# Attention and gated feed-forward on one core: the first chunk's attention and first feature steps in halves of 256 queries, and output stores ahead of transposes in SyncE's queue

## The chip, the core and the metric

The kernel runs on one NeuronCore of a Trainium2 chip. The metric is the device time of one execution in microseconds (us). Executions of one kernel agree within some 0.3%, so the effect here, about 1.2 us in 276, needs several runs of both kernels on the same chip. All numbers are from fast runs, unless a run is said to be a single one of unknown state.

## The reference

```python
scores = q @ k^T / 8                       # 4 batches, 8 heads, 768 positions, 64 per head
mask   = causal for heads 0, 2, 6 ("retrieval");
         the 4 first keys and a window of 64 for the other five ("streaming")
x      = softmax(scores) @ v               # -> 3072 tokens x 512
g, val = x @ w_gate, x @ w_val             # 512 -> 1536
y      = (gelu(g) * val) @ w_out           # 1536 -> 512
out    = x + sigmoid(x @ w_res) * y
```

## The kernel before

The 3072 tokens are worked in six chunks of 512. A chunk's attention makes `xT` (its output, transposed to features by tokens); then follow twelve feature steps f = 0 to 11, each with four gate and four value matmuls of 512 columns, GELU on ScalarE and a product on VectorE; then the output.

Nothing is ordered by hand. The program adds tasks with an engine, an assumed duration, dependencies and a priority (lower goes first), and a list scheduler, at build time, fixes the order of instructions on every engine. `HINTS` replaces priorities by task number; it was found by a search for this set of tasks, so its numbers mean something else as soon as a task is added. `.late` adds to the assumed landing time of a transfer: it changes no transfer, only the order that the scheduler chooses.

```python
P_ps = Psum(psum, {            # PSUM: 8 banks; kind: (slots at once, the banks of each)
    "av1": (2, one(0, 1)), "av2": (1, [(0, 1)]), "av0": (3, [(0, 1), (6, 7), (2, 3)]),
    ...
    "gv": (4, one(6, 7, 5, 4, 3, 2)), "gv0": (4, one(6, 7, 5, 4)), "gv00": (2, one(6, 7)), ...
})
P_ot = Pool(many("otile", 3, [128, D_MODEL], FP32))      # three output tiles
...
def load_weights():                                      # all issued on GpSimd's queue
    ...                                                  # wg, wv in 3 pieces: priority -20 + j
    wtok["r"] = dma("pool", -12, 2.6, ...)
    for j in range(4):
        wtok["o", j] = dma("pool", -11 + j, 1.95, ...)
...
def loads_rows(c, si, b, a, z):                          # chunks 0 and 1
    base = {0: -60, 1: -15, 2: 50}[c]
    ...                                                  # queries, keys: priority base + ...
    values(b, a, z, base + (10 if c == 0 else 8), False, c == 0)
...
# a chunk's feature steps: a matmul group needs all 512 queries
for f in range(NF):
    pr = 1000 * c + 500 + f
    kind = "gv" if f > 1 else "gv0" if c or f else "gv00"
    ...
# the store of an output tile, in SyncE's queue
G.add("sp", 0.6, ... e.dma_start(out[r0:r0 + 128, w], at(ot)[:, w]) ..., [t2], pr, bufs=[ot], dma=0.75, name="out")
...
# matmuls of a blank tile fill TensorE where nothing else is ready
G.add("pe", 0.06, ... e.matmul(at(warm)[:, 0:128], lhsT=blank[:, :], rhs=blank[:, :], ...), [t_blank], 1e9, ...)
...
for c, segs in enumerate(CHUNKS):
    attention(c, segs, xbuf, xtbuf, xtoks, xttoks)
    h, htoks = gate_value(c, xtbuf, xttoks)
    output(c, h, htoks, xbuf, xtoks, xtbuf, xttoks)
```

SyncE's queue also carries the transposes of later chunks' queries and keys, and the shift copies `vs <- va` (values moved by 64 rows for the window).

The softmax here doesn't subtract the row's maximum and nothing guards it: scores larger than these inputs give would overflow.

Of the kernel before, what the change touches and what calls it, by code (L numbers as in the profile page):

```python
# [42 lines left out]
    "3:-21.19 5:-58.49 6:-58.34 403:490.65 425:595.32 427:528.41 578:-99.99 586:59.9 611:1499.22 612:516.59 "  # L43
    "622:576.96 635:549.35 636:510.21 637:1538.66 643:580.14 647:570.57 648:558.53 649:1085.71 650:1520.19 "
    "653:525.88 654:576.91 655:1026.63 659:511.56 665:514.73 666:516.61 668:1537.73 671:15.77 673:62.65 "
    "677:0.03 679:80.17 680:-75.91 683:82.91 684:-86.3 685:102.37 686:529.24 689:511.01 701:88.3 702:-1.38 "
    "703:114.98 707:516.6 719:1104.93 722:2562.67 733:1538.65 734:1503.99 756:501.37 777:2386.85 816:2334.5 "
    "855:2510.01 861:1434.93 874:2134.02 886:2457.99 922:3352.32 923:1980.91 924:1487.38 972:2502.01 "
    "996:3513.25 1004:2538.32 1026:1534.33 1040:3534.81 1067:2441.52 1090:4509.27 1095:4498.99 1113:4499.01 "
    "1136:4429.99 1139:3502.04 1181:4467.35 1251:4123.82 1253:4130.53 1262:4510.02 1322:5341.74 1368:4505.02 "  # L50
    "1370:5425.02 1394:5537.53 1399:5528.12 1411:5499.01 1412:4524.63 1418:5505.02 1423:5573.53 1424:5090.24 "
    "1444:5424.01 1446:4529.17 1457:5122.53 1458:6525.69 1468:5116.43 1482:4952.05 1485:6442.5 1510:5505.99 "
    "1553:5511.01 1554:5505.99 1608:7485.06 1628:7447.37 1653:7483.11 "
# [391 lines left out]
def build_kernel(nc, q, k, v, w_gate, w_val, w_out, w_res, out):  # L445
# [34 lines left out]
        "av1": (2, one(0, 1)), "av2": (1, [(0, 1)]), "av0": (3, [(0, 1), (6, 7), (2, 3)]),  # L480
        "sc": (2, [(2, 3), (4, 5)]), "scr": (3, one(5, 4, 3, 2)), "scr0": (3, one(6, 5, 4, 3, 2)),
        "gv": (4, one(6, 7, 5, 4, 3, 2)), "gv0": (4, one(6, 7, 5, 4)), "gv00": (2, one(6, 7)), "out": (2, one(6, 7)), "warm": (1, one(7, 5, 1)),
# [56 lines left out]
    def load_weights():  # L539
        for j in range(3):  # L540
            for nm, t, src in (("g", wg, w_gate), ("v", wv, w_val)):
                s = slice(j * 512, (j + 1) * 512)
                wtok[nm, j] = dma("pool", -20 + j, 2.6, (lambda t=t, s=s: lambda: t[:, :, s])(),
                                  src[:, s].rearrange("(ci p) f -> p ci f", p=128))
        wtok["r"] = dma("pool", -12, 2.6, lambda: wr[:, :, :], w_res.rearrange("(ci p) f -> p ci f", p=128))
        for j in range(4):
            s = slice(j * 3, (j + 1) * 3)
            wtok["o", j] = dma("pool", -11 + j, 1.95, (lambda s=s: lambda: wo[:, s, :])(),
                               w_out[j * 384:(j + 1) * 384, :].rearrange("(fi p) c -> p fi c", p=128))

# [14 lines left out]
    def values(b, a, z, base, each, on_engines=False):  # L565
# [21 lines left out]
        if on_engines:  # L587
            ts = []
            for dst, src, off in ((0, 64, 1), (64, 0, 0)):
                def vs(on, dst=dst, src=src, off=off):  # L590
                    def fn(e):
                        o = at(BB.vs)[dst:dst + 64, a_ - 1:z - 1, :, :].rearrange("p i h d -> p (i h d)")
                        i_ = at(BB.v)[src:src + 64, a_ - off:z - off, :, :].rearrange("p i h d -> p (i h d)")
                        return e.activation(out=o, in_=i_, func=AF.Copy) if on == "act" else e.tensor_copy(out=o, in_=i_)
                    return fn
                n_ = (z - a_) * 520
                ts.append(G.flex({"dve": (c_dve(n_, 3.0, False), vs("dve")), "act": (c_act(n_), vs("act"))},
                                 [BB.vtok[i - off] for i in range(a_, z)], 130, bufs=[BB.v, BB.vs], name="vs"))
            for i in range(a_, z):
                BB.vstok[i] = ts  # L600
            late_copies.extend(ts)
            return
# [13 lines left out]
    def loads_rows(c, si, b, a, z):  # L616
# [18 lines left out]
        values(b, a, z, base + (10 if c == 0 else 8), False, c == 0)  # L635

        per = 1 if c == 0 or n == 4 else 2
        for k_ in range(0, NPAIR, per):
            ps_ = ORDER[k_:k_ + per]
            pr = 1000 * c - 492 + ps_[0] if c else 40 * k_ - 5  # L640
# [29 lines left out]
    def loads_natural(c, si, b, a, z):  # L670
# [5 lines left out]
        for i in range(a, z):  # L676
            for j, src in ((1, k), (0, q)):
# [6 lines left out]
                t = G.add("sp", 1.3, (lambda sv=sv, i=i, j=j: lambda e: e.dma_start(  # L684
# [11 lines left out]
    def attention(c, segs, xbuf, xtbuf, xtoks, xttoks):  # L696
        tiles = [(b, i) for (b, a, z) in segs for i in range(a, z)]
        todo = []
        for k_, p in enumerate(ORDER):
            P = B()  # L700
            P.heads, P.p, P.c, P.pr = PAIRS[p], p, c, 1000 * c + 40 * k_
# [23 lines left out]
        sinks = sink_scores(c, [t for t in tiles if t[1] > 0], 1000 * c + 40 + 5)  # L725
        for t in ph(c, "sc")[:-1]:
            if t.name[2:] in (str(ORDER[2]), str(ORDER[3])):
                t.order.append(ph(c, "sc")[-1])
# [9 lines left out]
        last, norms = None, []  # L738
        for P in todo:
# [3 lines left out]
            last, tn = weigh(P, tiles, sinks, xbuf, x16, xtoks, xdeps, last)  # L743
            if P.heads[0] % 2 == 1:
                for cb in (P.heads[0] // 2, P.heads[1] // 2):
                    to_features(c, cb, P.pr, x16, xdeps, xtbuf, xttoks)
                if P is todo[-1]:
                    tn.order += [t for _, t in xttoks[-2:]]
                if c == 0 and P is todo[-1]:
                    for t in norms[1:]:  # L750
                        t.order.append(xdeps[-1])
            norms.append(tn)

# [87 lines left out]
    def sink_scores(c, need, pr):  # L841

        S = B()
        S.where, S.four, S.et = {}, {}, Buf(P_ek)
        scr = Buf(P_ps, "sc")
        for m, (b, i) in enumerate(need):
            for h in (1, 3, 5, 7):
                S.where[h, b, i] = m * 128
            S.where[4, b, i] = 512
# [3 lines left out]
        cols = (need + need[-1:])[0:4]  # L853
# [13 lines left out]
        for j, (b, i) in enumerate(cols):  # L867
            mms.append((j, batch(b), slice(0, 64), 1, 512, i * 128, 128))

        def sc(e):  # L870
# [7 lines left out]
        S.txs = [G.add("act", c_act(640), lambda e: e.activation(  # L878
            out=at(S.et)[:, 0:640], in_=at(scr)[:, 0:640], func=AF.Exp, scale=SM_SCALE),
            [ts], pr, bufs=[scr, S.et], fset="exp", name="expk")]  # L880
# [3 lines left out]
    def weigh(P, tiles, sinks, xbuf, x16, xtoks, xdeps, last):  # L884
        n = len(tiles)
        c, pr, heads = P.c, P.pr, P.heads
        av = Buf(P_ps, "av2" if c else "av0")
# [3 lines left out]
        def windows(xs, lts):  # L891
            def fn(e):
                r = []
                for x in xs:
                    for lt in lts:
                        b, i = tiles[lt]
                        o, w, BB, h = x * 512 + lt * 65, P.where[x, None, b, i], batch(b), heads[x]
                        for s in range(2):
# [3 lines left out]
                                              start=lt == 0, stop=(i == 0), skip_group_check=True))  # L902
# [3 lines left out]
        def keys(x, lt):  # L906
            def fn(e):
                b, i = tiles[lt]
                o = x * 512 + lt * 65
                return [e.matmul(at(av)[:, o:o + 65], lhsT=at(P.et)[:, P.where[x, kt, b, i]:P.where[x, kt, b, i] + 128],  # L910
                                 rhs=at(batch(b).v)[:, kt, heads[x], :], start=lt == 0 and kt == 0, stop=(kt == i),
# [3 lines left out]
        def sinkf(x, h):  # L915
            def fn(e):
                r = []
                for lt, (b, i) in enumerate(tiles):
                    if i == 0:
                        continue  # L920
                    o, ko = x * 512 + lt * 65, sinks.where[h, b, i]
# [25 lines left out]
        def avv(d0, d1):  # L947
            return at(av).rearrange("p (x w) -> p x w", x=2)[:, :, 0:n * 65].rearrange(
# [8 lines left out]
        xview = lambda: at(xbuf)[:, 0:n, :].rearrange("p i (y x d) -> p x i y d", x=2, d=128)[:, :, :, heads[0] // 4, half]  # L957
        direct = c == 0 or heads[0] % 2
        if direct:

            xdeps.append(G.add("dve", c_dve(2 * n * 64), lambda e: e.tensor_tensor(
                out=at(x16)[:, :, :, half], in0=avv(0, DHEAD), in1=scale(), op=ALU.mult), [t1], pr - 2.5, bufs=[av, rc, x16], name="norm16"))
        t2 = G.add("dve", c_dve(2 * n * 64), lambda e: e.tensor_tensor(  # L963
            out=xview(), in0=avv(0, DHEAD), in1=scale(), op=ALU.mult), [t1] + xdeps, pr - 2 + (200 if c == 0 and heads[0] else 0), bufs=[av, rc, xbuf], name="norm")
        for i in range(n):
            xtoks.setdefault(i, []).append(t2)
        if not direct:
            def cast(on):
                return lambda e: (e.activation(out=at(x16)[:, :, :, half], in_=xview(), func=AF.Copy) if on == "act" else
                                  e.tensor_copy(out=at(x16)[:, :, :, half], in_=xview()))  # L970
# [4 lines left out]
    def to_features(c, cb, pr, x16, xdeps, xtbuf, xttoks):  # L975
        n = 4
# [5 lines left out]
        def ev(on):  # L982
            def fn(e):
                o, i_ = at(xtbuf)[:, cb, 0:n * 128], at16(scr)[:, 0:n * 128]
# [7 lines left out]
    def gate_value(c, xtbuf, xttoks):  # L992
# [4 lines left out]
        for f in range(NF):  # L997
            pr = 1000 * c + 500 + f
            kind = "gv" if f > 1 else "gv0" if c or f else "gv00"
# [20 lines left out]
            toks.append(th)  # L1020
# [3 lines left out]
    def output(c, h, htoks, xbuf, xtoks, xtbuf, xttoks):  # L1024
        segs = [(b, t) for (b, a, z) in CHUNKS[c] for t in range(a, z)]
        for lt in range(4):
# [14 lines left out]
            for w in ((slice(0, 256), slice(256, 512)) if last else (slice(0, 512),)):  # L1041
                fb = Buf(P_ps, "gv" if last else "out")
                n = w.stop - w.start
                for j in range(6):
# [3 lines left out]
                        [prev_t, wtok["o", j * 2 // 3], wtok["o", (2 * j + 1) // 3]] + htoks[2 * j:2 * j + 2], pr,  # L1048
# [6 lines left out]
                    [t1] + xtoks[lt], pr + (0 if c == len(CHUNKS) - 1 else 90), bufs=[ot, xbuf], name="add")  # L1055
                G.add("sp", 0.6, (lambda ot=ot, r0=r0, w=w: lambda e: e.dma_start(out[r0:r0 + 128, w], at(ot)[:, w]))(),
                      [t2], pr, bufs=[ot], dma=0.75, name="out")
# [13 lines left out]
    firsts = None  # L1071
    for t in late_copies:
        t.order += [x for d in (batches[0].ktok, batches[0].qtok) for (p, i), x in d.items() if i == 0]
    for c, segs in enumerate(CHUNKS):
        xbuf, xtbuf, xtoks, xttoks = Buf(P_x), Buf(P_xt), {}, []
        attention(c, segs, xbuf, xtbuf, xtoks, xttoks)
        firsts = firsts or xttoks
        h, htoks = gate_value(c, xtbuf, xttoks)
# [3 lines left out]
    for c in range(len(CHUNKS)):  # L1082
        gv, gelu = ph(c, "gv"), ph(c, "gelu")
        for f, t in gv:
            t.order += ph(c, "sc") + (ph(c, "xT") if f > (1 if c else 0) else [])
        for t in ph(c, "table"):
            t.order += ph(c, "exp") + ([x for _, x in firsts[:2]] if c == 0 else [])
# [65 lines left out]
```

## Time and profile before

| what | before | where it is read |
|---|---|---|
| median of 3 runs | 275.91 us (275.73 to 276.66) | run times |
| profiled span | 274.1 us | page |
| TensorE busy, 8.7 to 21.9 us | 12.52 of 13.2, of which blank 6.14 | windows |
| first feature matmul | 21.92 us | TensorE's timeline |
| TensorE's waits at the end of chunk 1's attention | 0.69 + 0.47 us | TensorE's timeline |

How to read it: TensorE is nearly always busy, so a saving must come from one of the few stretches where its work is blank or where it waits. There are two: the start, before the first feature step, and 67 to 70 us. The lines are in the prediction.

### The profile page before, as it was taken

Reading aid. Unit: us, or ns where it says so; the run is one execution under the profiler, and the core shown is the slowest. Engines: PE = TensorE matmul, PEld = TensorE weight load, DVE = VectorE, ACT = ScalarE, POOL = GpSimd, SP = SyncE. Lnnn points to the kernel's source line nnn. Section 1 sums busy time; section 2 is a strip of 40 time slices with the busy share of each in tenths; the row PEclk is TensorE's granted clock in tenths of the full one; section 3 lists DMA queues with packets and bytes.
Section 4 is the critical chain, followed back from the end, with each engine's and each line's share of the span. In section 5 each row is a group of like instructions: output and inputs, shape, how many; then the busy total and the mean of one; then the engine's idle time right before and its main releaser. Section 6 shows DMA issues by size and latency. Waiting matters only on the chain.

```text
span 274.1 us, 5645 instructions
## 1 busy us (share of the span) xinstructions
PE 267.2 (97%) x2398; PEld 138.5 (51%) x2398; DVE 139.6 (51%) x254; ACT 140.7 (51%) x205; POOL 86.2 (31%) x120
## 2 busy tenths in 40 slices
PE   7999999999999999999999999999999999999995
PEld 7774454454444465444455444455444456544443
DVE  2785353386433457435456544467525156743344
ACT  3744266775435876434773333776333778333410
POOL 8999259991382532992000000000000000000000
PEclk9999999999999999999999999999999999999999
DMA  6999999999999999999911000121100011200022
GB/s 88 174 206 207 184 207 177 146 201 129 166 148 146 249 132 211 156 155 147 191 41 41 2 38 0 41 77 42 41 0 0 1 42 39 79 0 0 0 77 80
DMA packets 92474, 27.81 MB, mean 101 GB/s; under 512 B 81184, under 2 KB 88864, under 8 KB 92448
## 3 DMA queue, kind: packets, MB, share of 16 engines
q0 software_dynamic: 70320, 14.69, 68.3%
q1 hardware_dynamic: 22128, 12.76, 23.6%
q8 instruction: 19, 0.31, 0.5%
q14 instruction: 7, 0.06, 0.1%
HBM read 29.36 MB, written 6.29 MB: 130 GB/s over the span
## 4 chain that ended last, share of the span: by engine, by line
PE 92%; DMA 2%; POOL 2%; DVE 1%; issue 1%; ACT 1%; POOLq 0%
PE ps L1003 45%; PE ps L1046 23%; PE ps L1031 8%; PE ps L783 5%; PE ps L910 3%; DMA va<-in_v_dram 2%; PE ps L900 2%; PE ps L978 2%; PE ps L924 2%; POOL qks L535 1%; PE ps L1062 1%; PE ps L646 1%; DVE hT L1017 1%; PE ps L871 1%; ACT xT L985 0%
## 5 line engine op out<-in xcount | busy, mean ns | idle before, releaser
L1017 DVE SCALAR_TENSOR_TENSOR hT<-gact,ps 128x512 f16<-128x512 f16 x72 | 48.7, 687 | 72.6 <-ACT gact L1015 48.2
L1015 ACT ACTIVATE gact<-ps 128x512 f16<-128x512 f32 x72 | 42.8, 597 | 72.0 <-PE ps L1003 65.9
L1003 PE MATMUL ps<-xT,wg 128*128 128x512 f16 x288 | 78.6, 380 | 0.5 <-ACT xT L985 0.5
L1003 PE MATMUL ps<-xT,wv 128*128 128x512 f16 x288 | 78.8, 379 | 0.0
L1046 PE MATMUL ps<-wo,hT 128*128 128x512 f16 (+1 forms) x300 | 70.4, 371 | 0.0
L1003 PEld LDWEIGHTS ps<-xT,wg 128*128 128x128 f16 x288 | 27.7, 98 | 33.7 <-ACT xT L985 0.6
L1003 PEld LDWEIGHTS ps<-xT,wv 128*128 128x128 f16 x288 | 27.9, 98 | 33.4 <-DVE hT L1017 0.4
L1046 PEld LDWEIGHTS ps<-wo,hT 128*128 128x128 f16 x300 | 27.0, 98 | 27.5 <-issue 1.5
L799 ACT ACTIVATE er<-ps 128x1024 f16<-128x1024 f32 (+3 forms) x40 | 34.8, 903 | 9.8 <-PE ps L783 9.6
L535 POOL DMA_DIRECT2D qks<-in_k_dram x36 | 28.4, 834 | 31.2 <-DMA qkt<-qks 23.3
L535 POOL DMA_DIRECT2D qks<-in_q_dram x36 | 29.0, 858 | 0.8 <-POOLq L1135 0.8
L1050 DVE SCALAR_TENSOR_TENSOR otile<-srs,ps 128x512 f32<-128x512 f32 (+1 forms) x25 | 16.5, 661 | 24.2 <-PE ps L1046 24.1
L1031 PE MATMUL ps<-wr,xT 128*128 128x512 f16 x96 | 24.6, 380 | 0.0
L535 POOL DMA_DIRECT2D va<-in_v_dram x24 | 21.3, 940 | 6.6 <-PE ps L924 6.6
L1034 ACT ACTIVATE srs<-ps 128x512 f32<-128x512 f32 x24 | 14.3, 597 | 12.3 <-PE ps L1031 12.1
L783 PE MATMUL ps<-qkt 64*128 64x64 f16 (+4 forms) x396 | 17.2, 215 | 0.1
L1053 DVE TENSOR_TENSOR otile<-otile,xtok 128x512 f32<-128x512 f32 (+1 forms) x25 | 16.6, 665 | 0.6
L963 DVE TENSOR_TENSOR xtok<-ps,rcp 128x512 f32<-128x512 f32 x24 | 16.4, 687 | 0.5
L985 ACT ACTIVATE xT<-ps 128x512 f16<-128x512 f16 x12 | 6.8, 596 | 15.3 <-PE ps L978 15.3
L783 PEld LDWEIGHTS ps<-qkt 64*128 64x128 f16 x396 | 10.3, 95 | 7.8 <-issue 3.2
L1031 PEld LDWEIGHTS ps<-wr,xT 128*128 128x128 f16 x96 | 8.4, 98 | 9.9 <-issue 0.7
L799 ACT ACTIVATE es<-ps 128x1024 f16<-128x1024 f32 x12 | 12.3, 1021 | 2.1 <-PE ps L783 2.0
(59 smaller groups left out, 195.6 us busy)
## 6 DMA issues: line engine op xcount, KB each, us to landing
out_dram<-otile SPq DMA_DIRECT2D x23, 256.0 KB, 2.2
va<-in_v_dram POOLq DMA_DIRECT2D x24, 128.0 KB, 18.1
qks<-in_k_dram POOLq DMA_DIRECT2D x32, 64.0 KB, 17.1
qks<-in_q_dram POOLq DMA_DIRECT2D x32, 64.0 KB, 16.8
wg<-in_moe_w_gate_dram POOLq DMA_DIRECT2D x3, 512.0 KB, 10.1
wv<-in_moe_w_val_dram POOLq DMA_DIRECT2D x3, 512.0 KB, 12.0
wo<-in_moe_w_out_dram POOLq DMA_DIRECT2D x4, 384.0 KB, 22.4
vs<-va SPq DMA_DIRECT2D x4, 260.0 KB, 5.3
```

Source lines behind the costliest of these rows:

```text
L535: return G.add(eng, issue, lambda e: e.dma_start(out_ap(), in_ap), deps, prio, bufs=bufs, dma=cost, name=name, grp=grp)
L783: return [e.matmul(at(scr)[:, oo:oo + w], lhsT=at(BB.qkt)[half, 1, p, k0:k0 + 128], rhs=at(BB.qkt)[half, 0, p, qq:qq + w], start=True, sto ...
L799: return e.activation(out=o, in_=i_, func=AF.Exp, scale=SM_SCALE)
L963: t2 = G.add("dve", c_dve(2 * n * 64), lambda e: e.tensor_tensor(out=xview(), in0=avv(0, DHEAD), in1=scale(), op=ALU.mult), [t1] + xdeps, ...
L1003: return lambda e: [e.matmul(at(dst)[:, :], lhsT=w[:, ci, f * 128:(f + 1) * 128], rhs=at(xtbuf)[:, ci, :], start=(ci == 0), stop=(ci == NC ...
L1015: ta = G.add("act", c_act(512), (lambda gb=gb, ga=ga: lambda e: e.activation(out=at(ga)[:, :], in_=at(gb)[:, :], func=AF.Gelu))(), [tg], p ...
L1017: th = G.add("dve", c_dve(512), (lambda vb=vb, ga=ga, f=f: lambda e: e.scalar_tensor_tensor(out=at(h)[:, f, :], in0=at(ga)[:, :], scalar=0 ...
L1031: e.matmul(at(rb)[:, :], lhsT=at(xtbuf)[:, ci, s], rhs=wr[:, ci, :], start=(ci == 0), stop=(ci == NCB - 1))
L1034: ta = G.add("act", c_act(512), (lambda rb=rb, sr=sr: lambda e: e.activation(out=at(sr)[:, :], in_=at(rb)[:, :], func=AF.Tanh, scale=0.5)) ...
L1046: e.matmul(at(fb)[:, w], lhsT=at(h)[:, fi, s], rhs=wo[:, fi, w], start=(fi == 0), stop=(fi == NF - 1))
L1050: t1 = G.add("dve", c_dve(n), (lambda fb=fb, sr=sr, ot=ot, w=w: lambda e: e.scalar_tensor_tensor(out=at(ot)[:, w], in0=at(sr)[:, w], scala ...
L1053: t2 = G.add("dve", c_dve(n), (lambda ot=ot, lt=lt, w=w: lambda e: e.tensor_tensor(out=at(ot)[:, w], in0=at(ot)[:, w], in1=at(xbuf)[:, lt, ...
```

## The change

The intent: the first half of chunk 0's queries goes through attention first, and its first four feature steps run while the second half is still in attention. The stores of the output get a priority that puts them ahead of the transposes in SyncE's queue. The search for hints was run anew.

```diff
-    "3:-21.19 5:-58.49 6:-58.34 403:490.65 ...            (HINTS, cut)
+    "0:-35.76 3:-22.77 399:-347.39 ... 743:-165.05 ...    (HINTS, cut)
-        "av1": (2, one(0, 1)), "av2": (1, [(0, 1)]), "av0": (3, [(0, 1), (6, 7), (2, 3)]),
+        "av1": (2, one(0, 1)), "av2": (1, [(0, 1)]), "av1": (3, one(0, 1, 6)),
-        ... "gv00": (2, one(6, 7)), ...
+        ... "gvh": (4, one(7, 6, 4, 5)), ...
+            wtok["o", j].late = 2.2
 ...                                    (not shown: other bank lists, chunk 0's priorities, two rules of order)
 ...                                    (chunk 0's shift copies: 2 tasks become 4)
-        values(b, a, z, base + (10 if c == 0 else 8), False, c == 0)
+        values(b, a, z, base + (10 if c == 0 else 2), False, c == 0)
 ...                                    (assumed time of a transpose: 1.3 becomes 1.65)
 ...                                    (weighing, normalising, transposing: for n = 2 tiles too)
+            if f < len(halves) * 2:
+                for hf, deps in enumerate(halves):
+                    s = slice(256 * hf, 256 * hf + 256)
+                    gb, vb, ga = Buf(P_ps, "gvh"), Buf(P_ps, "gvh"), Buf(P_ga)
+                    ...                 (4 gate and 4 value matmuls of 256 columns,
+                    ...                  GELU and product of 256 columns)
+                continue
 ...
-                      [t2], pr, bufs=[ot], dma=0.75, name="out")
+                      [t2], pr - 3000, bufs=[ot], dma=0.75, name="out").late = 3.0
 ...
-        attention(c, segs, xbuf, xtbuf, xtoks, xttoks)
+        if c == 0:
+            last, ek = None, Buf(P_ek)
+            for l0 in (0, 2):
+                halves.append([])
+                last = attention(c, [(0, l0, l0 + 2)], xbuf, xtbuf, xtoks, halves[-1], l0, last, ek)
+                xttoks.extend(halves[-1])
+        else:
+            attention(c, segs, xbuf, xtbuf, xtoks, xttoks)
```

The offset of `values` goes from 8 to 2 for chunk 1.

## The prediction

> **What bounds the kernel now.** I read the page's busy shares first, then a table of windows, then each engine's timeline of the first 25 us, because the change touches chunk 0 only (and the store queue).
>
> ```profile
> PE 267.2 (97%) x2398; PEld 138.5 (51%) x2398; DVE 139.6 (51%) x254; ACT 140.7 (51%) x205; POOL 86.2 (31%) x120
> ...
> 8.70:21.90 13.20, 12.52 (x268) 9.92 (x264) 11.66 (x27) 9.05 (x12) 13.20 (x20) 1.00 1.59 192
> ...
> 70.00:271.00 201.00, 200.99 (x1587) 98.65 (x1584) 100.00 (x176) 101.61 (x149) 31.90 (x42) 1.00 0.67 76
> ```
>
> The second and third lines are windows: length, then busy time of PE, PEld, DVE, ACT, POOL, then clock, DMA share, GB/s. From 70 to 271 us TensorE never stops, so nothing hidden beside it there can pay. The stretch before 21.9 us also looks full, but the same view for the warm-up line alone (columns PE, PEld) says what fills it:
>
> ```profile
> 8.70:21.90 13.20, 6.14 (x76) 4.38 (x76) 1.00 1.59 192
> ```
>
> 76 of its 268 matmuls multiply a blank tile, and they are busy 6.14 of 13.2 us. TensorE has room here. What it waits for is in the timelines of TensorE and VectorE around the first feature step (start, length, engine, line):
>
> ```profile
> 19.57 0.50 PE L1062 MATMUL ps<-blank 128*128 128x128 f16 x6
> 19.90 0.61 PE L978 MATMUL ps<-ident,x 128*128 128x128 f16 x8
> 20.98 0.45 PE L1062 MATMUL ps<-blank 128*128 128x128 f16 x5 [0.47 <-ACT xT L985]
> 21.27 0.61 PE L978 MATMUL ps<-ident,x 128*128 128x128 f16 x8
> ...
> 24.09 3.62 PE L1003 MATMUL ps<-xT,wv 128*128 128x512 f16 x16
> 27.54 2.75 PE L1003 MATMUL ps<-xT,wg 128*128 128x512 f16 x12
> ```
>
> ```profile
> 17.66 0.68 DVE L963 TENSOR_TENSOR xtok<-ps,rcp 128x512 f32<-128x512 f32 x1
> 18.26 0.27 DVE L950 RECIPROCAL rcp<-ps 128x8 f32<-128x8 f32 x2
> 18.49 0.69 DVE L961 TENSOR_TENSOR x<-ps,rcp 128x512 f16<-128x512 f32 x1
> 19.76 0.21 DVE L950 RECIPROCAL rcp<-ps 128x8 f32<-128x8 f32 x1 [0.58 <-PE ps L924]
> 19.89 1.24 DVE L961 TENSOR_TENSOR x<-ps,rcp 128x512 f16<-128x512 f32 x2
> 21.04 0.68 DVE L963 TENSOR_TENSOR xtok<-ps,rcp 128x512 f32<-128x512 f32 x1
> 21.69 0.76 DVE L985 COPY xT<-ps 128x512 f16<-128x512 f16 x2
> ```
>
> The first gate matmul starts at 21.92 us. VectorE is 11.66 of 13.2 us busy and ends the stage: weighing, normalisation, transposes, copies. ScalarE is done with the exponentials at 17.0 us. From 21.92 us on, matmuls run back to back: the 16 of the value group are 27.54 - 24.09 = 3.45 us apart, 0.216 us each.
>
> **What the Trainium skill says.** "TensorE: Matmul & The Clock Gate", Back-to-back issue gap, gives N/2.4 + 2.5 ns: 216 ns for 512 columns, 109 ns for 256. The trace agrees: 0.216 us above, and the 23 spacings of 256-column matmuls in the last output tile average 109 ns. So halves cost TensorE nothing; their weight loads are hidden. "VectorE: DVE Perf Modes", The TRN2 errata, says that small operands pay a fixed cost per instruction. Here: L1050, fp32 from PSUM, takes 683 ns at 512 and 417 ns at 256 elements, so two halves are 0.15 us dearer than one whole; adjoining ones overlap (1.24 us for two above), leaving about 0.1 us. "ScalarE: Activation LUTs", What ACT_TABLE_LOAD costs, gives 186 ns + 0.833 ns per element; the trace has 592 ns for 512 and 1023 ns for 1024, a fixed part near 0.16 us. Its table load of 1283 ns is in the trace as 1.28 us, at 21.43 us.
>
> **The change part by part.** (1) Queries 0-255 go through attention first, then 256-511. (2) Feature steps run by half while their number is below twice the number of halves: f = 0 to 3, four gate and four value groups of four matmuls per half. (3) A half's accumulators need one bank, not two; three slots. (4) Stores get priority -3000. (5) New scheduling hints.
>
> *Gained on TensorE.* First-half work: 4 x 8 matmuls x 0.109 = **3.5 us**, which may run in place of blank matmuls while VectorE works on the second half. Limits: the landing times. The first gate and value weights were issued at 9.99 and 11.00 us.
>
> ```profile
> DMA to landing us min/median/max: 6.8/10.1/13.7
> ...
> DMA to landing us min/median/max: 8.3/12.0/15.5
> ```
>
> (Gate weights, then value weights; their minima belong to the first pieces.) They land near 16.8 and 19.3 us. Value work of any half can't start before 19.3 us. The second pieces, needed by f = 4, land near 21.9 and 24.5 us, in time for a step that began at 28.8 us (21.92 + 32 x 0.216). Also, GELU waits for its table, and so for the last exponential of the second half, and the halves have four banks: steps 0 and 1 of half one fill them until GELU and the product (VectorE, 0.42 us) release them.
>
> *Paid on ScalarE.* The exponentials keep their 7040 columns but become 15 instructions instead of 8, as I count them from the banks: 7 x 0.16 = 1.1 us. They end near 18.1 instead of 17.0 us; there are 3.3 us idle behind them, so this hides behind VectorE.
>
> *Paid on VectorE, ahead of the second half's last copy.* Four more fp16 normalisations 4 x 0.1 = 0.4; five more masks, about 0.08 each, 0.4; four more reciprocals at 0.13 (two in 0.27 us above), 0.5; two more shift copies 0.2; with three accumulator slots for eight pair-halves, at least five fp32 normalisations of 0.38 must come first, 1.9 us, where the old kernel did two of 0.64, so 0.6 more. Sum 2.1 us. Two products of half one may add up to 0.8. Against it: idle gaps of about 0.6 us can be filled, and half-size tails (mask, normalise, transpose, copy at 256) save about 0.4 us of latency. Net, the second half is ready about **1.7 us later**, near 23.8 us instead of 22.1.
>
> *Sum.* f = 4 starts at 23.8 + 3.5 = 27.3 instead of 28.8 us: **-1.5 us** if all of half one's work fits in before; -0.6 if only steps 0 and 1 fit well (1.7 us).
>
> *Later.* The one stall that TensorE has after the start is at the end of chunk 1's attention:
>
> ```profile
> 68.58 0.61 PE L978 MATMUL ps<-ident,x 128*128 128x128 f16 x8 [0.69 <-DVE x L961]
> 69.66 1.04 PE L1003 MATMUL ps<-xT,wg 128*128 128x512 f16 x4 [0.47 <-ACT xT L985]
> ```
>
> 1.2 us in all. New hints may shrink or enlarge it; I take 0.3 us of gain as its mean, a guess.
>
> *Stores.* Their queue before:
>
> ```profile
> 52.05 0.38 SPq L1056 DMA_DIRECT2D out_dram<-otile  x1
> ...
> 70.46 15.53 SPq L684 DMA_TRANSPOSE qkt<-qks  x8
> 86.04 1.59 SPq L1056 DMA_DIRECT2D out_dram<-otile  x3
> ```
>
> Three stores of chunk 0 do stand behind chunk 3's transposes until 86.04 us. But no VectorE instruction waited for an output tile: line L1050's idle time was all put down to TensorE. And chunk 2's transposes are issued by 69.7 us while its scores come after 88 us. So I put this part at **0 us**.
>
> Taking 1.3 us for the start (between 0.6 and 1.5, nearer the latter) and 0.3 us for the later stall: 275.9 - 1.6 = **274.3 us**.
>
> **The rivals.** *A: VectorE becomes the whole bound.* It is already 88% busy; if the halves cost it 3 to 3.5 us rather than 1.7, the gain is eaten: 275.5 to 276.5 us. For it: the added instructions and the products that compete. Against: about 0.6 us of its time was idle, and ScalarE can take copies. *B: the halves hide well.* If the second half is ready at 22.3 us, the whole 3.5 us counts: 272.6 us, and 271.5 with the later stall gone. Against: value weights at 19.3 us leave only 3 us for 3.5 us of work. *C: the saved time is lost later*, because DMA is busy up to 85 us and chunk 1 arrives no sooner: its queries and keys landed just before their transposes at 35.84 us. For it: share 1.88 in the window 21.9 to 67. Against: those transposes have feature steps to hide behind, and its first weighing at 57.6 us comes some 8 us after its values. If so, 275.5 to 276 us. *D: stores ahead block transposes*, because the queue works in order. Slack of over 12 us speaks against it.
>
> **Range and chances.** B gives the low end, A and C the high end; 272.6 to 276.0 us should hold 8 times in 10. Faster by over 2% would need 270.4 us, more than the 3.5 us and the 1.2 us together: 3%. Slower by over 2% would need a new stall of 5.5 us: 1%. Within 2%: 96%.
>
> **What would show it.** Gate matmuls of 256 columns should begin at 17 to 20 us among second-half attention, with fewer blank ones; the last copy of the second half should end near 23.8 us; f = 4 should start near 27.3 us. VectorE should be over 90% busy from 8.7 to 23 us. The stores should leave before 70 us with nothing gained from it. The stretch after 70 us should only shift. I am wrong if value work starts far later than 19.3 us, if TensorE idles between the halves, or if a new gap shows up in chunk 1.

## The result, and the profile after

| kernel | median | runs | profiled span |
|---|---|---|---|
| before, same rounds | 276.02 us (275.73 to 276.66) | 4 | 274.1 us |
| after | 274.83 us (274.58 to 275.01) | 4 | 273.0 us |
| after, once more on another chip (before there: 276.09) | 274.96 us (274.44 to 275.84) | 6 | – |

The ratio is 0.9953, 95% interval 0.9933 to 0.9973: within 2%. (A ratio is the mean time of one kernel's fast runs over that of the other's in the same rounds, so not quite the ratio of the medians.) So 1.2 us were gained. The question is where.

First the page's busy line, then windows of the kernel after: length, then PE, PEld, DVE, ACT, POOL, clock, DMA share, GB/s.

```profile
PE 266.8 (98%) x2413; PEld 140.7 (52%) x2413; DVE 141.5 (52%) x275; ACT 144.0 (53%) x222; POOL 85.8 (31%) x120
...
8.70:21.90 13.20, 13.10 (x254) 9.87 (x248) 11.34 (x37) 11.77 (x23) 13.20 (x21) 1.00 1.57 190
64.00:70.00 6.00, 6.00 (x54) 3.13 (x53) 3.30 (x7) 2.16 (x6) 4.74 (x6) 1.00 1.64 165
```

The last window for the kernel before:

```profile
64.00:70.00 6.00, 4.83 (x72) 2.78 (x70) 4.10 (x9) 2.31 (x4) 2.38 (x3) 1.00 1.76 131
```

Before, TensorE is busy 4.83 of the 6 us from 64 to 70; after, all 6.00. That alone is 1.17 us. VectorE in the first window is busy 11.34 of 13.2 us, no more than before; ScalarE took the extra load, 11.77 against 9.05. The blank matmuls alone, in that same first window of the kernel after (length, PE, PEld, clock, DMA share, GB/s):

```profile
8.70:21.90 13.20, 6.22 (x62) 3.83 (x62) 1.00 1.57 190
```

They are drawn as busy for 6.22 us, against 6.14 before, although there are 62 of them instead of 76. In a run the blank ones start 0.056 us apart, but a lone one is drawn 0.22 us long, because ends are modelled; so busy time overstates short runs. By that spacing blank work fell by some 0.8 us (an estimate: 14 x 0.056). The first half's features were to take the place of 3.5 us of it. TensorE's timeline after (start, length, engine, line) says why they took so little:

```profile
19.61 0.22 PE L1100 MATMUL ps<-blank 128*128 128x128 f16 x1
...
20.50 0.60 PE L1022 MATMUL ps<-xT,wv 128*128 128x256 f16 x4
20.94 1.04 PE L1022 MATMUL ps<-xT,wg 128*128 128x256 f16 x8
21.81 0.22 PE L941 MATMUL ps<-vk,ek 128*128 128x65 f16 x2
...
23.62 0.22 PE L917 MATMUL ps<-vs,es 128*64 128x65 f16 x1
...
25.32 0.39 PE L994 MATMUL ps<-ident,x 128*128 128x128 f16 x4
...
27.30 0.61 PE L1040 MATMUL ps<-xT,wg 128*128 128x512 f16 x2 [0.30 <-DMA wg<-in_moe_w_gate_dram]
```

The first half's features (L1022) begin at 20.50 us, only 1.4 us before the whole chunk's began in the old kernel (21.92), and the last blank matmul started at 19.61. From 20.5 us on, features of the first half and attention of the second (L917, L941) take turns. The second half's last transposes (L994) run at 25.32; before, the whole chunk's ran at 21.27. So by the time the first half is ready, no blank matmul is left to replace; its features can only fill gaps between the pieces of the second half.

A second reading needs a sum of my own. For every matmul that is not blank I count N/2.4 + 2.5 ns (at least 25), the formula of the Trainium skill that the prediction cites and that both traces agree with (512 columns 0.216 us, 256 columns 0.109 us apart). It is an estimate, but one that tells how much of TensorE's real work is still to be done at a moment:

| at us | left before | left after | after less before |
|---|---|---|---|
| 18 | 255.31 | 256.48 | +1.17 |
| 20 | 254.60 | 255.47 | +0.87 |
| 22 | 253.76 | 253.69 | -0.07 |
| 26 | 249.88 | 249.92 | +0.04 |
| 28 | 247.72 | 248.40 | +0.68 |
| 64 | 209.37 | 210.13 | +0.76 |
| 70 | 205.36 | 204.07 | -1.29 |
| 268 | 2.83 | 1.75 | -1.08 |

In halves, attention alone falls 1.2 us behind by 18 us; the first half's features bring it level by 22 and no further; by 28 us it is 0.7 us behind again, part of it the wait for gate weights at 27.30 us. Single traces differ, so I made the same sum for others. Five more with the halves (after_again, a_g9, a_g9_again, a_vals8, a_unstore) stand at +1.1 to +1.8 us against the kernel before at 18 us and at -0.2 to +0.7 at 22; two with the whole chunk (b_vals_wo, whole) at +0.2 to +0.4 and at 0 to +0.1. No trace shows a lead worth the name at the start. At 64 us the new kernel is still behind. All that it gains, it gains from 64 to 70 us, and from there the lead only stays. The totals, 264.66 us before and 264.76 after, say that the amount of real work is the same.

### The profile page after: what moved, and what is told of

It reads as the page before. It is cut to its first block, busy times and chain, and to the rows that moved or that the text cites. A ratio compares the mean times of both kernels' runs of the same rounds, so it can differ in the third digit from the quotient of the medians.

```text
span 273.0 us, 5729 instructions
## 1 busy us (share of the span) xinstructions
PE 266.8 (98%) x2413; PEld 140.7 (52%) x2413; DVE 141.5 (52%) x275; ACT 144.0 (53%) x222; POOL 85.8 (31%) x120
## 3 DMA queue, kind: packets, MB, share of 16 engines
q1 hardware_dynamic: 22128, 12.76, 23.8%
## 4 chain that ended last, share of the span: by engine, by line
PE 89%; DMA 5%; POOL 4%; issue 1%; DVE 0%; POOLq 0%
PE ps L1040 43%; PE ps L1083 23%; PE ps L1068 8%; DMA wg<-in_moe_w_gate_dram 5%; PE ps L794 5%; PE ps L927 3%; PE ps L917 2%; PE ps L994 2%; PE ps L941 1%; PE ps L1022 1%; POOL qks L540 1%; POOL va L540 1%; PE ps L653 1%; PE ps L885 1%; POOL wg L540 1%
## 5 line engine op out<-in xcount | busy, mean ns | idle before, releaser
L1054 DVE SCALAR_TENSOR_TENSOR hT<-gact,ps 128x512 f16<-128x512 f16 x68 | 45.6, 686 | 65.2 <-ACT gact L1052 33.8
L1052 ACT ACTIVATE gact<-ps 128x512 f16<-128x512 f32 x68 | 40.4, 597 | 66.7 <-PE ps L1040 57.5
L1040 PE MATMUL ps<-xT,wg 128*128 128x512 f16 x272 | 73.3, 379 | 0.3 <-DMA wg<-in_moe_w_gate_dram 0.3
L1040 PE MATMUL ps<-xT,wv 128*128 128x512 f16 x272 | 73.3, 379 | 0.0
L1040 PEld LDWEIGHTS ps<-xT,wg 128*128 128x128 f16 x272 | 26.2, 98 | 31.2 <-DMA wg<-in_moe_w_gate_dram 0.6
L1040 PEld LDWEIGHTS ps<-xT,wv 128*128 128x128 f16 x272 | 26.3, 98 | 30.7 <-ACT gact L1052 0.4
L810 ACT ACTIVATE er<-ps 128x1024 f16<-128x1024 f32 (+4 forms) x40 | 34.4, 891 | 7.3 <-PE ps L794 6.9
L1071 ACT ACTIVATE srs<-ps 128x512 f32<-128x512 f32 x24 | 14.3, 596 | 17.0 <-PE ps L1068 16.9
L980 DVE TENSOR_TENSOR xtok<-ps,rcp 128x512 f32<-128x512 f32 (+1 forms) x28 | 16.9, 608 | 0.5
L1001 ACT ACTIVATE xT<-ps 128x512 f16<-128x512 f16 (+1 forms) x19 | 9.8, 538 | 12.6 <-PE ps L994 12.6
L1100 PE MATMUL ps<-blank 128*128 128x128 f16 x118 | 11.2, 241 | 2.6 <-DVE blank L514 2.6
```

The source lines that it names most:

```text
L810: return e.activation(out=o, in_=i_, func=AF.Exp, scale=SM_SCALE)
L980: t2 = G.add("dve", c_dve(2 * n * 64), lambda e: e.tensor_tensor(out=xview(), in0=avv(0, DHEAD), in1=scale(), op=ALU.mult), [t1] + xdeps, ...
L1040: return lambda e: [e.matmul(at(dst)[:, :], lhsT=w[:, ci, f * 128:(f + 1) * 128], rhs=at(xtbuf)[:, ci, :], start=(ci == 0), stop=(ci == NC ...
L1052: ta = G.add("act", c_act(512), (lambda gb=gb, ga=ga: lambda e: e.activation(out=at(ga)[:, :], in_=at(gb)[:, :], func=AF.Gelu))(), [tg], p ...
L1054: th = G.add("dve", c_dve(512), (lambda vb=vb, ga=ga, f=f: lambda e: e.scalar_tensor_tensor(out=at(h)[:, f, :], in0=at(ga)[:, :], scalar=0 ...
L1071: ta = G.add("act", c_act(512), (lambda rb=rb, sr=sr: lambda e: e.activation(out=at(sr)[:, :], in_=at(rb)[:, :], func=AF.Tanh, scale=0.5)) ...
```

## The experiments

Three theories, and I held the first one when I predicted. **Halves**: the 1.2 us come from chunk 0's features hidden in attention. **Values**: they come from chunk 1's values being asked for earlier. **Stores**: they come from the store priority.

### The values' place in the queue: undone alone, and done alone

a_vals8 is the kernel after with the old offset; b_vals is the kernel before with the new one.

```diff
 a_vals8 (on after)
-        values(b, a, z, base + (10 if c == 0 else 2), False, c == 0)
+        values(b, a, z, base + (10 if c == 0 else 8), False, c == 0)
 b_vals (on before): the reverse
```

> The changed kernel with the values' offset back at 8, all else kept. Theory V: a stall of 1 to 3 us returns near 62 to 70 us, time 1.2 to 2.8 us over the changed kernel, 276 to 277.6 us, no better than before. Rival H: still 274.5 to 275.3 us.

> The kernel before, with one number changed: chunk 1's values are asked for ahead of the residual and output weights (offset 2 instead of 8), nothing else, hints as before. Theory V (the gain comes from chunk 1's values landing earlier, which takes away TensorE's stall of 1.2 us at 67 to 70 us; the halves net nothing): values land near 37 to 40 us instead of 47 to 50, the stall at 67 to 70 us is gone, time 1.2 to 1.8 us under before, that is 274.2 to 274.8 us, as fast as the changed kernel. Rival H (the halves at the start make the gain): at most 0.3 us under before.

a_vals8: 277.78 us, ratio to before 1.0062 (1.0046 to 1.0078): 3 us slower than the kernel after, and slower than before although it has the halves and the stores. In its TensorE timeline the waits at the end of chunk 1's attention are back:

```profile
70.32 0.61 PE L994 MATMUL ps<-ident,x 128*128 128x128 f16 x8 [0.68 <-DVE x L978]
71.39 1.47 PE L1040 MATMUL ps<-xT,wg 128*128 128x512 f16 x6 [0.47 <-ACT xT L1001]
```

The same two lines of the kernel after carry no wait and stand 4 to 5 us earlier:

```profile
66.22 0.61 PE L994 MATMUL ps<-ident,x 128*128 128x128 f16 x8
66.67 1.03 PE L1040 MATMUL ps<-xT,wg 128*128 128x512 f16 x4
```

The landing times in the traces agree: chunk 1's values land at 36.8 to 39.8 us after (46.7 to 49.7 before) and its shift copies at 42.4 to 44.9 us (54.9 to 58.1 before). The output weights pay for it: the last piece lands at 50.3 us, not 45.5.

b_vals: 276.04 us, ratio 0.9994 (0.9979 to 1.0009): nothing gained. The stall is gone in its profile (TensorE busy 8.00 of the 8 us from 64 to 72; 6.83 before), but the time comes back elsewhere: waits for the output weights between 49 and 52 us (0.35 and 0.88 us in the timeline), and waits for feature weights before 26.3 us (0.89 and 0.42 us), which landed later in that execution. It was the slowest of the six, 276.98 us, so the waits for feature weights may not be typical. So the new offset is what removes the stall, and a kernel whose order of instructions was made for the old landing times loses as much at the weights.

### The wait for gate weights

In the kernel after one hint moves the gate matmuls of step 9 forward, to the weights' third piece that has not landed. a_g9 takes that hint away; a_g9_again repeats it beside the unchanged kernel after_again on one chip.

```diff
-    "743:-165.05 746:2404.58 749:533.58 ...
+    "746:2404.58 749:533.58 ...
```

> The changed kernel without the one hint that puts gate step 9 in front of everything at 27 us, where its weights have not landed. Theory: the wait of 0.3 us (0.47 us of spacing) for the gate weights at 26.7 to 27.3 us goes, first matmuls after the halves run on at once, time 0.4 to 0.5 us under the changed kernel, 274.3 us. Rival: the saved time turns up as a wait elsewhere (the next pieces of weights, or chunk 1), then no change.

> The changed kernel again, so that it is timed on the same chip as the other runs of this call. 274.6 to 275.0 us; its lead over the kernel before 1.0 to 1.4 us.

> The changed kernel without the one hint for gate step 9, beside the changed kernel on the same chip. If the wait for gate weights at 27 us reached the end: 0.3 to 0.5 us under it. If not: within 0.15 us.

a_g9: 274.98 us, ratio 0.9953 (0.9939 to 0.9968), the same as after. The wait was gone in its profile, whose span was 272.4 us, but the timed runs show no gain. Side by side: after_again 274.96 us (0.9955), a_g9_again 275.00 us (0.9960). So this wait of 0.3 us is worth nothing that 6 runs each can show. The profiled execution of a_g9_again began its exponentials 0.76 us later than that of after_again (9.57 against 8.81 us), which says how far one profiled execution is from another at the start; a difference of half a microsecond between two single profiles should not be explained.

### The stores

```diff
 a_unstore (on after)
-                      [t2], pr - 3000, bufs=[ot], dma=0.75, name="out").late = 3.0
+                      [t2], pr, bufs=[ot], dma=0.75, name="out")
```

> The changed kernel with the stores' priority and their extra landing time back as before. As predicted blind: no gain or loss from the stores themselves, within 0.5 us of the changed kernel. Rival S: without it stores wait in front of chunk 2's transposes, these come late, and TensorE waits for chunk 2's scores near 87 to 95 us, 2 to 5 us slower.

286.84 us, ratio 1.0384 (1.0362 to 1.0405): 12 us slower. The queue of SyncE in a_unstore, with its first stores in the last line:

```profile
70.32 19.81 SPq L691 DMA_TRANSPOSE qkt<-qks  x8
...
98.82 8.39 SPq L1094 DMA_DIRECT2D out_dram<-otile  x5
```

The same queue in the kernel after:

```profile
57.01 1.11 SPq L1094 DMA_DIRECT2D out_dram<-otile  x2
...
62.96 0.59 SPq L1094 DMA_DIRECT2D out_dram<-otile  x1
...
70.86 0.59 SPq L1094 DMA_DIRECT2D out_dram<-otile  x1
```

And what that does, from the table of waits of a_unstore (us in total, times, longest):

```profile
DVE otile L1087 <- DMA out_dram<-otile: 6.1, 1, 6.1
...
PE ps L1068 <- DVE otile L1087: 5.3, 1, 5.3
```

The first stores of full output tiles go out at 98.82 us. VectorE waits 6.1 us for a tile, until 103.56 us, and TensorE waits 5.3 us for VectorE to empty a bank. Three more waits of TensorE (1.3, 0.8 and 1.8 us) fall at 89 to 98 us; each is put down to an exponential on ScalarE. These waits make 9.3 us. Afterwards TensorE is busy but slow (window: length, PE, PEld, DVE, ACT, POOL, clock, DMA share, GB/s):

```profile
105.00:110.00 5.00, 5.00 (x31) 2.08 (x30) 1.85 (x4) 1.91 (x3) 5.00 (x8) 0.59 2.00 222
```

The granted clock is 0.50 from 100 to 105 us and 0.59 here, and from 104.3 to 107.3 us matmuls of 512 columns start 0.427 us apart instead of 0.216. So the stall costs more than its length: by work left the kernel loses 11.9 us between 80 and 120 us, some 2.6 more than the waits.

The Trainium skill ("DMA: Bandwidth & Descriptors", Anatomy of one DMA — SWDGE (gpsimd) path, in a sentence on DMA engines in general) says that the semaphore wait of a transfer happens on the issuing sequencer before dispatch; this run agrees in effect: whatever stands behind a waiting transpose in SyncE's queue stays there, here until 98.82 us. My prediction of no gain from the stores fits the kernel before, where no VectorE instruction waited for a tile; no run adds the priority alone to that kernel. It was no reason to think them dispensable: in this order of instructions they are worth 12 us as a guard.

### The old attention with the other changes

If the halves are worth nothing, the whole chunk with the other changes should be as fast as after. Three kernels try it.

```diff
 b_vals_wo (on before)
+            wtok["o", j].late = 2.2
-        values(b, a, z, base + (10 if c == 0 else 8), False, c == 0)
+        values(b, a, z, base + (10 if c == 0 else 2), False, c == 0)
 whole: the same, and
-                      [t2], pr, bufs=[ot], dma=0.75, name="out")
+                      [t2], pr - 3000, bufs=[ot], dma=0.75, name="out")
 whole_retuned: the same, .late = 3.0 on the stores and 1.5 on two thirds of wg and wv,
   1.65 for a transpose, and hints from a search on the scheduler's own assumed times
```

> The kernel before with chunk 1's values first, as in b_vals, and with the scheduler told that the output weights land 2.2 us later, as the changed kernel has it; no halves, no store priority, hints as before. Theory V: the waits for output weights at 49 to 51 us (1.6 us in b_vals) shrink by 1 us or more, the stall at 67 to 70 us stays away, time 274.5 to 275.3 us. Rival H (only the halves pay): 275.8 us or more.

> The kernel before (whole chunk 0, its own hints) with three of the changed kernel's other parts: chunk 1's values first, output weights told to land 2.2 us later, stores at priority -3000. No halves. Theory V (values first makes the gain, the halves net nothing, and the store priority is what lets it stand): the 10 us wait of b_vals_wo is gone, no stall at 67 to 70 us, time 274.5 to 275.3 us, within 0.3% of the changed kernel. Rival H: 275.8 us or more.

> The same, with the later landing of the weight pieces for steps 4 to 11 told to the scheduler too, transposes at 1.65 us as in the changed kernel, and hints found anew for this structure by a random search on the scheduler's own times. It asks whether whole chunks are held back by hints made for another order. Theory V: 274.3 to 275.3 us, level with the changed kernel within 0.3%. Rival: the halves are worth their modelled part, then 0.5 us or more behind the changed kernel.

b_vals_wo: 287.27 us, ratio 1.0387 (1.0358 to 1.0416). The sum of work left is 0.86 us ahead of the kernel before at 80 us (194.57 against 195.43). Then one stall takes 10 us, again from stores behind transposes:

```profile
DVE otile L1051 <- DMA out_dram<-otile: 11.1, 1, 11.1
...
PE ps L1004 <- DVE otile L1051: 10.0, 1, 10.0
```

The clock falls here too: from 92.87 to 98.4 us matmuls of 512 columns start 0.427 us apart. By work left the kernel loses 13.0 us between 80 and 120 us, 3.0 more than the stall.

whole: 277.36 us, ratio 1.0050 (1.0023 to 1.0076). That stall is gone with the store priority, and so is chunk 1's (TensorE busy 8.00 of 8 us from 64 to 72). At 70 us it is 0.64 us ahead of the kernel before by work left (204.72), half of what the kernel after has. It then loses it in new waits, the largest of them in chunk 2's features, for a free bank:

```profile
130.72 0.60 PE L1004 MATMUL ps<-xT,wg 128*128 128x512 f16 x2 [1.43 <-DVE hT L1018]
```

whole_retuned: 281.39 us, ratio 1.0178 (1.0153 to 1.0204, a verdict of unclear). A search on the scheduler's own times made it worse: TensorE waits 3.0 us for shift copies, until 63.0 us, and then runs at a lower clock, 0.60 in the next window, though it is busy throughout:

```profile
65.00:70.00 5.00, 5.00 (x42) 2.60 (x41) 2.38 (x5) 1.08 (x2) 0.00 (x0) 0.60 1.99 170
```

So whole-chunk attention can have the gain at 64 to 70 us too, but no version of it that I built kept the gain to the end. That the halves are dispensable is not shown; neither is that they are needed, since none of these kernels had hints found on the chip for its own set of tasks.

### What sets the second half's end

I had predicted that VectorE sets it. Three kernels, all wrong, take one suspect each away: the masks of chunk 0 on 8 of 128 columns (a_maskcut), the exponentials of chunk 0 on a quarter of their columns (a_expcut), and three of four matmuls of each group in the first half's features (a_thin).

```diff
 a_maskcut
-  ... out=split(view()), in0=split(view()), in1=m_, op=ALU.mult ...
+  cut = 8 if P.c == 0 else 128
+  ... out=split(view())[..., 0:cut], in0=split(view())[..., 0:cut], in1=m_[..., 0:cut], op=ALU.mult ...
 a_expcut
+  q = 4 if P.c == 0 else 1
-  o, i_ = at(P.et)[:, o0:o0 + cols], at(scr)[:, 0:cols]
+  o, i_ = at(P.et)[:, o0:o0 + cols // q], at(scr)[:, 0:cols // q]
   ...                                   (and er, es filled with ones at the start)
 a_thin
-  start=(ci == 0), stop=(ci == NCB - 1)) for ci in range(NCB)])(),
+  start=(ci == 0), stop=(ci == (NCB if hf else 1) - 1)) for ci in range(NCB if hf else 1)])(),
```

> Wrong result on purpose: the changed kernel with chunk 0's ten mask multiplications cut to 8 of every 128 columns, same instructions in the same order. It takes about 2.5 us of VectorE's work out of the stage. Theory: VectorE bounds the second half, so its last copy ends 1.5 us or more before 26.0 us. Rival: the second half is bound by TensorE's order (first-half features stand in front of its weighing) or by the exponentials; then its last copy moves by less than 0.7 us. The whole time then moves by at most as much, limited by the gate weights that land at 27.3 us.

> Wrong result on purpose: the changed kernel with chunk 0's exponentials cut to a quarter of their columns (the rest of their tiles is filled with ones while VectorE is idle at 2.5 to 6 us), same instructions in the same order on every engine. It takes some 4 us of ScalarE's work out of the stage. If ScalarE's longer row of exponentials makes the second half late: its last copy ends 1.5 us or more earlier against the first half's start of work (26.0 us, or 6.0 us after the first half's last copy, in the changed kernel). If only TensorE's order does: less than 0.5 us. The total should gain at most what the gate weights at 27.3 us leave, under 1 us.

> Wrong result on purpose: the changed kernel with each first-half gate and value group cut from four matmuls to one, so 2.6 us of TensorE work is gone from between the second half's weighings; all else the same. If the features in front of the second half's weighing delay it: last copy 1 us or more before 26.0 us. If VectorE or ScalarE bounds it: less than 0.5 us earlier. The total is not compared, because work is missing.

I read the spacing from the first half's last copy on VectorE to the second half's, because the executions start at different moments. The kernel after:

```profile
19.73 0.28 DVE L1001 COPY xT<-ps 128x256 f16<-128x256 f16 x1
...
25.74 0.29 DVE L1001 COPY xT<-ps 128x256 f16<-128x256 f16 x1 [0.17 <-PE ps L994]
```

a_maskcut:

```profile
20.50 0.28 DVE L1002 COPY xT<-ps 128x256 f16<-128x256 f16 x1
...
26.50 0.29 DVE L1002 COPY xT<-ps 128x256 f16<-128x256 f16 x1 [0.17 <-PE ps L995]
```

a_expcut:

```profile
29.35 0.28 DVE L1002 COPY xT<-ps 128x256 f16<-128x256 f16 x1
...
35.36 0.29 DVE L1002 COPY xT<-ps 128x256 f16<-128x256 f16 x1 [0.16 <-PE ps L995]
```

a_thin:

```profile
19.62 0.28 DVE L1001 COPY xT<-ps 128x256 f16<-128x256 f16 x1
...
24.43 0.28 DVE L1001 COPY xT<-ps 128x256 f16<-128x256 f16 x1
```

6.01 us in the kernel after, 6.00 with 2.0 us less of masks on VectorE (their ten rows sum to 1.63 instead of 3.63 us), 6.01 with 4.0 us less of exponentials on ScalarE (4.11 instead of 8.11 us), and 4.81 with 24 matmuls x 0.109 = 2.6 us less of features on TensorE. So neither the masks nor the exponentials set how long the second half ends after the first; the features in TensorE's order do, for 1.2 us of it. (VectorE's other work was not cut.) All 32 half-size matmuls of the first half (3.5 us) lie in that order ahead of the second half's last transposes, and by work left TensorE does 5.55 us of real work in the 6 us from 20 to 26 us. Of the 2.6 us taken away only 1.2 come through, since TensorE now waits for others: in a_thin's timeline 0.18 us for a mask, 0.17 for a GELU, 0.32 for a normalisation.

a_thin shows a second thing. With three quarters of the first half's features gone, the second half's last copy still ends at 24.71 us, 2.3 us after the whole chunk's in the kernel before (22.45), and the exponentials of both began at nearly the same time (8.89 and 8.76 us). So the features taken out explain 1.3 us of the 3.6 us by which the second half is late. The other 2.3 us remain with 0.9 us of features still there; at least some 1.4 us (an estimate, 2.3 - 0.9) must come with attention in halves itself.

The whole times say little. a_maskcut took 274.92 us (0.9938, 0.9904 to 0.9971; relative error 0.27). a_thin took 275.25 us in a single run of unknown state; once the second half was early it waited 1.0 us for gate weights, until 27.04 us. Its result passed the comparison, but it leaves out products that the reference has, so it is no correct kernel. a_expcut took 283.61 us (1.0253; relative error 0.29): filling `er` and `es` with ones delayed the start by some 8 us, and the clock was 0.50 to 0.59 between 10 and 20 us, so it is read only for its spacing, which lies where the clock was 1.00 again (25 to 36 us).

## Why the prediction was right and wrong

The total was right: 274.3 us predicted, 274.83 measured, inside the range and within 2%. Its working was mostly wrong, and two errors nearly cancelled: the hit was luck.

- **"-1.3 us at the start": measured about 0.** The step that failed is "the second half is ready about 1.7 us later", near 23.8 us, because VectorE bounds it. It was ready at 26.03 us, 3.6 us later than the whole chunk before (22.45). The term was mis-sized and its mechanism was at least incomplete: I added up VectorE's instructions and never asked in which order TensorE takes its own. The first half's 3.5 us of features stand in front of the second half's last transposes; with 2.6 us of them taken out, the last copy ended 1.3 us earlier, while 2.0 us less of masks on VectorE did not bring it closer to the first half. The other 2.3 us, already above my 1.7, remain with attention in halves and 0.9 us of features; no run parts them. My starting point was off too: 22.1 us stands in no line, the whole chunk's last copy ended at 22.45. The steps of 512 columns (f = 4 and later) began in pieces from 25.54 us, but with first steps of the second half still to do: by work left, the new kernel was level at 26 us.
- **The 3.5 us were to replace blank matmuls.** That there was blank work was right, though 6.14 us was its drawn length: 76 matmuls 0.056 us apart are 4.3 us. That the first half could use it was not checked. It can only if the half is ready while there is blank time. It was ready at 20.2 us, and the last blank matmul started at 19.61. My own limit, "value work can't start before 19.3 us" (it began at 20.50), should have warned me: before that moment lay nearly all the blank work.
- **VectorE over 90% busy: no**, 11.34 of 13.2 us in the window 8.7 to 21.9, and 12.27 of 14.3 up to 23 us, both 86%. The scheduler moved copies to ScalarE, whose last exponential ended at 19.92 us, not near 18.1. The exponentials themselves went from 7.19 to 8.11 us in the trace, 0.9 more for 1.1 predicted; most of the rest is four copies on ScalarE among them instead of one.
- **"0.3 us of gain as its mean, a guess" for the later stall: measured 2.05 us** by work left between 64 and 70 us (from 0.76 behind to 1.29 ahead). The prediction saw the stall and named its size, 1.2 us, but called what would become of it a matter of luck with hints. The line of the diff that removes it was there to be read.
- **Rival C, "the saved time is lost later", with the remark that chunk 1's first weighing "comes some 8 us after its values"**: the remark misled me. The shift copies of those values, which landed at 54.9 to 58.1 us, were near the weighing at 57.6 us; I had looked at the values and not at the copies behind them. The rival itself was partly true: from 26 to 64 us the new kernel fell 0.7 us further behind.
- **Stores: 0 us against before, not contradicted,** but not tested alone; the stores of chunk 0 left at 57 to 71 us, the last of the first four at 70.86 and so just after the 70 us predicted. That they are a guard worth 12 us in the new order was not foreseen.
- **Halves cost TensorE nothing per matmul: right**, 0.109 us each (8 in 20.94 to 21.81), and the stretch after 70 us only shifted, from 1.29 to 1.08 us of lead.

What stays open: why attention in halves is 1.2 us behind by 18 us. ScalarE's added 2.7 us in the window is the plain suspect, but in a_expcut the first half took 12.5 us from its first exponential to its last copy, against 11.1 in the kernel after, with the exponentials cut to a quarter. That run's start, with a clock of 0.50 to 0.59, differs too much to settle it. Open as well is whether whole-chunk attention with hints found on the chip would equal the kernel after.

## What to carry to other kernels

Filler on an engine is room for other work only if that work is ready while the filler runs: compare the two moments before adding up lengths, and remember that split work goes into the same instruction order as the part that it should overlap. Read every line of a diff for what it does to the order of transfers: undoing one changed priority of a load cost 3 us here, while the feature that the change was named for brought no lead of its own at the start. And test a "worth nothing" part by removing it from the new kernel, not only by asking what it gained on the old one.

## What the Trainium skill lacked or had wrong

- "TensorE: Matmul & The Clock Gate", Back-to-back issue gap: it gives N/2.4 + 2.5 ns for an isolated matmul and says that a real kernel sustains some 131 ns at 512 columns. Here streams of 512 columns with a weight load each ran 216 ns apart (16 in 3.45 us) and of 256 columns 109 ns apart: the formula holds inside the stream, and the 131 ns were not seen.
- "VectorE: DVE Perf Modes", Zero memsets can be issued as uint32, says that a memset takes one cycle per element. a_expcut agrees by the spacing of starts, 4.81 us for 4608 fp16 elements (5.64 to 10.45 us; 4.80 at the 0.96 GHz that the page's Specifications give), but the record of each such instruction shows 3.90 us, with 0.91 us of idle time just before it (0.91 and 0.16 us for 1024 elements). No page warns that a memset's row is shorter than its cost.
- No page has what a queue of transposes costs a store behind it: 8 transposes held SyncE's queue for 13.8 to 19.9 us here, their waits included, and the two kernels in which full output tiles waited behind them took 11 us longer (b_vals_wo than before) and 12 us longer (a_unstore than after), some 3 us of each after the waits, at a lower clock.
